# Decode block kernel: first feed-forward and query stage by halves of the heads, a third key tile loaded before it, spare matmuls between output projections, last part of the down weights in two

## The chip, the cores and the metric

One core of one Trainium2 chip runs the whole kernel in one launch. The metric is device time in microseconds (us), less is better. The engines named below: PE (matrix multiply), DVE (vector), ACT (activation), POOL (general), SP (here it only issues loads). PSUM is the memory that PE writes its sums to, in eight banks; SBUF holds everything else.

## The reference, cut to what matters

Four sequences, one new token each, pass twice through an attention block A and a feed-forward block B, with the same weights and the same cache both times.

```python
B, Sq, D = 4, 1, 512;  Hq, Hkv, Sk, Dh = 32, 8, 4096, 128;  F = 1792   # bf16

def A(x):                                  # x is the normalised input
    q = heads(x @ wq)                      # 32 query heads, 4 for each of 8 key heads
    s = q @ k_cache.T * Dh ** -0.5         # 4096 cached keys per key head
    return merge(softmax(s) @ v_cache) @ wo

def Bf(x):
    return (gelu(x @ w_gate) * (x @ w_up)) @ w_down

x = x + A(layernorm(x));  x = x + Bf(layernorm(x))
x = x + A(layernorm(x));  x = x + Bf(layernorm(x))
```

A key head's cache of one sequence is 1 MB, its values another; the kernel reads about 100 MB in all.

## The kernel before, in words

**Tiles.** A key or value tile is half of one head's cache of one sequence, 128 partitions by 16 x 128 numbers, 512 KB. The eight key heads are two groups of four; a group has 8 key tiles (4 heads, t = 0 and 1). SBUF has room for the 16 key tiles of one sequence (`KP`, line 93, in pairs of heads: `kp{g}_{t}_{j}`) and for 8 value tiles (`slots`, line 95). The key tiles of a sequence stay for both of its passes: what was loaded for pass 1 is used again, turned in place, in pass 2 of the same sequence, and only then overwritten with the next sequence's keys.

**Order of the work.** `attend_first` (873) does pass 1 of sequence 0, reads the other weights and does the output projection. Then, for b = 0 to 3, the loop at 1242 does the first feed-forward of sequence b (`dense_first` for b = 0, `dense` after), the queries of its second pass, and `attend(b + 1)` (946), in which pass 2 of sequence b and pass 1 of sequence b + 1 share the engines: scores of the two groups of pass 2 (`sc2`), softmax, values; in between the new keys land, DVE turns them (`Keys.turn`, 483), and the scores of pass 1 (`sc1`) follow, then the remaining values, the output projection (`RowProj`, `OutProj`), and the next feed-forward, in which the remaining values of pass 2 are filled in between (`Streamed`, `prev.fill`).

**Scores** (524). Four heads are computed side by side in four column strips of PE, 32 matmuls of 512 columns for a group: for each t, four parts (`be`) by four heads. They need `qb` (113), a spread-out copy of the queries: `q_sums` (305) makes 16 small matmuls with slices of the identity into PSUM, `q_spread` (314) writes the result times a mask to SBUF on DVE.

**Loads.** All are issued by SP in program order, and a load that overwrites a tile waits for the instructions that still read it. So new keys can be loaded only when the scores of pass 2 have read the old ones, and values only when a slot is free (`VRing.pump`, 628, called around each value step of `Values.step`, 748). An instruction with a wait holds back everything behind it on its engine.

**Around the change.** After the loads of the output, gate, up and down weights (`load_rest`, 139; the down weights in three parts of 6, 5 and 3 of 14 rows, `WD_PARTS`) one pair of new keys (sequence 1, first two heads of the first group, t = 0) is loaded ahead of the feed-forward. To make room, one pair of the second group's t = 1 tiles (`KP[gy2][1][1]`, heads 2 and 3) is copied by DVE into four free PSUM banks (`Parked`, 490; four copies). In `attend`, after the scores of t = 0, ACT copies half of it back to the pair of tiles that these scores have freed, and the other half after the softmax; `KP`'s entries are exchanged. The remaining new keys of the first group are loaded in pairs, one pair after t = 0, two after t = 1; the second group's 8 tiles one by one after its scores (985).

`dense_first` (1109): gate sums (56 matmuls), gelu, up sums (56), product, down sums (56 matmuls in 14 rows). `busy(n)` (439) issues n spare matmuls of 512 columns whose output (`idle`, in the bank of the scores) nobody reads: 6 before the up sums, 4 after, 2 before each later part of the down weights, 1 after the down sums, 1 after the queries and 1 after their sums. The queries of the first group are 64 matmuls (`q_proj`, 249), rounded by DVE (`q_round`, 298); those of the second group are computed after the first softmax (`qy`, 1300).

Of the kernel before, what the change touches and what calls it, by code (L numbers as in the profile page):

```python
# [15 lines left out]
P = 128  # L16
# [13 lines left out]
WD_PARTS = (0, 6, 11, 14)  # L30
# [3 lines left out]
def kernel(  # L34
# [80 lines left out]

    def k_tile(i, t):
        return KP[i // GH][t][i % GH // 2][:, i % 2]

    def acc(shape, name):
        t = ps_ac.tile([P, 512], FP32, name=name, tag="acc")  # L120
        n = 1
        for s in shape:
            n *= s
        if len(shape) == 1:
            return t[:, :n]
        return t[:, :n].rearrange("p (a b) -> p a b", b=shape[1])
# [171 lines left out]
    def q_round(q_bf, q, g, norm):  # L298
        nc.vector.scalar_tensor_tensor(out=q_bf[:], in0=cs_q[:, g], scalar=norm.mean,  # L299
# [4 lines left out]

    def q_sums(q):
        qe = ps_sm.tile([P, GH, BE, rep], FP32, name="qe", tag="sm")
        iv = ident_bf[:].rearrange("p (b w e) -> p b e w", b=NB, e=2)
        for be in range(BE):
            for a in range(QD):
                nc.tensor.matmul(qe[a * QS:(a + 1) * QS, :, be], lhsT=iv[:, be // 2, be % 2],  # L310
                                 rhs=q, start=True, stop=True, skip_group_check=True)
        return qe

    def q_spread(qe):
        dst = qb[:, W:].rearrange("p (n x a h) -> p n x a h", x=2, a=QD, h=rep)[:, :, 0]
        nc.vector.tensor_tensor(  # L316
            out=dst,
            in0=qe.rearrange("p s n h -> p (s n) h").unsqueeze(2).broadcast_to([P, NK, QD, rep]),
            in1=amask.unsqueeze(1).unsqueeze(3).broadcast_to([P, NK, QD, rep]),
# [12 lines left out]
    class OutProj:  # L332


        def __init__(self, o_of, nb):
            self.o, self.nb, self.n = o_of, nb, 0
            self.full = acc([KD, WIDE], "y")
# [49 lines left out]
    def ffn_in(rhs, w_sb, name):  # L387
        g = acc([KF, WIDE], name)
# [48 lines left out]
    idle = []  # L437

    def busy(count):
        if not idle:  # L440
            idle.append(ps_sc.tile([P, 512], FP32, name="idle", tag="sc"))
        for _ in range(count):
            nc.tensor.matmul(idle[0][:], lhsT=ident_bf[:], rhs=wg_sb[:, 0, :512], start=True,
                             stop=True, skip_group_check=True)

    def down(nb, H_bf):
        y = acc([KD, WIDE], "y2")
        for c in range(KF):
            if c in WD_PARTS[1:]:
                busy(2)  # L450
# [6 lines left out]
    class Keys:  # L457
# [16 lines left out]
        def load_pairs(self, count, into=None):  # L474
            for _ in range(count):
                kvh, t = self.tile(self.nl)
                self.nl += 2
# [863 lines left out]
```

## Time and profile before

| | us |
|---|---|
| median of three runs (272.24 to 274.52) | 273.4 |
| the profiled execution, its own time | 271.11 |
| its span, first to last instruction | 269.2 |
| PE busy | 190.0 |
| DVE busy | 174.7 |
| ACT busy | 64.2 |
| POOL busy | 2.7 |
| bytes moved | 103.08 MB, mean 383 GB/s |

How to read it: times in rows are microseconds from the span's start, then the duration, the engine, the line of the kernel (L531 is line 531; a helper's line stands for all its callers), the output and its inputs, the shape, and how often. What stands in brackets is how long the engine was idle before, and what ended that. PEld are weight loads of PE, which overlap its matmuls; SPq is SP's queue of load issues. A row of a stretch of time gives PE, PEld, DVE, ACT and POOL busy time with counts, then the granted clock of PE (1.00 is full), the share of the DMA engines that was busy, and the rate in GB/s. Transfers were above 90% busy in nearly all of the span; PE's clock was granted at full or at half speed, 0.854 on average.

### The profile page before, as it was taken

Reading aid. Unit: us, or ns where it says so; the run is one execution under the profiler, and the core shown is the slowest. Engines: PE = TensorE matmul, PEld = TensorE weight load, DVE = VectorE, ACT = ScalarE, POOL = GpSimd, SP = SyncE. Lnnn points to the kernel's source line nnn. Section 1 sums busy time; section 2 is a strip of 40 time slices with the busy share of each in tenths; the row PEclk is TensorE's granted clock in tenths of the full one; section 3 lists DMA queues with packets and bytes.
Section 4 is the critical chain, followed back from the end, with each engine's and each line's share of the span. In section 5 each row is a group of like instructions: output and inputs, shape, how many; then the busy total and the mean of one; then the engine's idle time right before and its main releaser. Section 6 shows DMA issues by size and latency. Waiting matters only on the chain.

```text
span 269.2 us, 8883 instructions
## 1 busy us (share of the span) xinstructions
PE 190.0 (71%) x3943; PEld 113.8 (42%) x3943; DVE 174.7 (65%) x428; ACT 64.2 (24%) x125; POOL 2.7 (1%) x8
## 2 busy tenths in 40 slices
PE   1395255634597896968869969687788786788893
PEld 1333133633364443544426335454354354453561
DVE  3394952130124799875676999566759995768863
ACT  1001000100404412030422610304137113044640
POOL 2000000000000000000000000000000000000001
PEclk9999559555599798687897997889979979799999
DMA  6999999999993999999999999999999999999940
GB/s 244 421 417 421 418 420 416 413 382 402 411 360 100 419 415 418 420 418 416 402 386 417 417 420 417 416 422 416 412 417 415 417 419 417 416 391 386 417 159 3
DMA packets 32430, 103.08 MB, mean 383 GB/s; under 512 B 2692, under 2 KB 8584, under 8 KB 32392
## 3 DMA queue, kind: packets, MB, share of 16 engines
q1 hardware_dynamic: 32368, 102.51, 95.1%
q8 instruction: 31, 0.51, 0.7%
q14 instruction: 7, 0.06, 0.1%
q10 hardware_dynamic: 24, 0.01, 0.0%
HBM read 102.50 MB, written 0.00 MB: 381 GB/s over the span
## 4 chain that ended last, share of the span: by engine, by line
DMA 51%; DVE 21%; PE 17%; SPq 6%; issue 2%; ACT 1%; DVEq 0%; ACTq 0%
DMA v_t<-in_A_v_cache_dram 29%; DMA kp<-in_A_k_cache_dram 13%; DVE kp L488 10%; PE sc L531 7%; DMA wu_sb<-in_B_w_up_dram 5%; DMA kp<-in_A_v_cache_dram 4%; SPq L142 4%; PE so L712 2%; DVE pe L541 2%; DVE q L280 2%; DVE qb L316 1%; PE ot L779 1%; PE y L246 1%; PE q L274 1%; SPq L143 1%
## 5 line engine op out<-in xcount | busy, mean ns | idle before, releaser
L488 DVE STREAM_TRANSPOSE kp<-kp 128x1024 f32<-128x1024 f32 x64 | 74.0, 1206 | 0.2 <-issue 0.2
L531 PE MATMUL sc<-kp,qb 128*32 128x512 bf16 x512 | 66.6, 449 | 7.5 <-DVE qb L316 2.5
L779 PE MATMUL ot<-pe,v_t 128*128 128x32 bf16 x1120 | 35.3, 181 | 14.4 <-DMA v_t<-in_A_v_cache_dram 12.4
L779 PEld LDWEIGHTS <-v_t 128*128 128x128 bf16 x1120 | 33.1, 99 | 24.2 <-DMA v_t<-in_A_v_cache_dram 15.9
L531 PEld LDWEIGHTS <-qb 128*32 128x32 bf16 x512 | 21.3, 102 | 42.2 <-issue 23.1
L553 ACT ACTIVATE pe<-sc,nl 128x512 bf16<-128x512 f32 x8 | 5.5, 687 | 84.9 <-DVE pe L550 67.2
L583 PE MATMUL x<-pe,ident_bf 128*32 128x128 bf16 x192 | 6.0, 255 | 15.1 <-DVE pe L561 15.0
L583 PEld LDWEIGHTS <-ident_bf 128*32 128x32 bf16 x256 | 5.6, 107 | 18.9 <-issue 17.1
L541 DVE TENSOR_REDUCE pe<-sc 128x1 f32<-128x512 f32 x12 | 8.3, 689 | 7.9 <-PE sc L531 7.9
L720 DVE STREAM_TRANSPOSE so<-so 128x256 f32<-128x256 f32 (+1 forms) x19 | 11.1, 584 | 3.2 <-PE so L712 3.1
L712 PE MATMUL so<-v_t,pe 128*32 128x256 bf16 x192 | 10.2, 341 | 2.8 <-ACT pe L586 1.4
L246 PE MATMUL y<-OT_bf,wo_sb 128*128 128x32 bf16 x192 | 7.3, 190 | 6.8 <-DMA wo_sb<-in_A_wo_dram 6.7
L246 PEld LDWEIGHTS <-wo_sb 128*128 128x128 bf16 x256 | 8.6, 102 | 8.0 <-DMA wo_sb<-in_A_wo_dram 7.1
L586 ACT CAST pe<-x 128x512 bf16<-128x512 f32 x12 | 7.0, 585 | 20.3 <-PE x L583 20.3
L712 PE MATMUL so<-v_t,pl 128*32 128x256 bf16 x192 | 9.7, 283 | 2.9 <-DMA v_t<-in_A_v_cache_dram 2.6
L379 DVE TENSOR_TENSOR xb<-XX,y 128x4 bf16<-128x4 f32 (+1 forms) x9 | 1.6, 173 | 14.2 <-PE y L246 14.1
L246 PE MATMUL q<-xb,wq_sb 128*128 128x5 bf16 (+1 forms) x192 | 5.4, 170 | 7.3 <-DMA wq_sb<-in_A_wq_dram 7.3
L561 DVE STREAM_TRANSPOSE pe<-pe 128x512 bf16<-128x512 bf16 x12 | 8.4, 697 | 3.2 <-ACT pe L553 3.2
L616 DVE TENSOR_TENSOR OT_bf<-ot,rden 128x8 bf16<-128x8 f32 (+1 forms) x20 | 3.0, 156 | 11.1 <-PE ot L779 11.0
L360 PE MATMUL yr<-wo_sb,OT_bf 128*2 128x512 bf16 (+1 forms) x96 | 10.2, 494 | 0.0
L310 PE MATMUL qe<-q_bf,ident_bf 128*32 128x16 bf16 x256 | 4.4, 175 | 8.2 <-DVE q_bf L299 6.3
L712 PEld LDWEIGHTS <-pe 128*32 128x32 bf16 x208 | 6.1, 113 | 8.2 <-issue 3.8
(148 smaller groups left out, 229.6 us busy)
## 6 DMA issues: line engine op xcount, KB each, us to landing
v_t<-in_A_v_cache_dram SPq DMA_DIRECT2D x97, 512.0 KB, 8.9
kp<-in_A_k_cache_dram SPq DMA_DIRECT2D x40, 512.0 KB, 12.4
kp<-in_A_k_cache_dram SPq DMA_DIRECT2D x12, 1024.0 KB, 8.3
wq_sb<-in_A_wq_dram SPq DMA_DIRECT2D x2, 2048.0 KB
wo_sb<-in_A_wo_dram SPq DMA_DIRECT2D x4, 1024.0 KB, 11.4
wq_sb<-in_A_v_cache_dram SPq DMA_DIRECT2D x3, 1024.0 KB, 11.2
wg_sb<-in_B_w_gate_dram SPq DMA_DIRECT2D x1, 1792.0 KB
wu_sb<-in_B_w_up_dram SPq DMA_DIRECT2D x1, 1792.0 KB
```

What stands on the lines that cost most here:

```text
L142: dq.dma_start(out=wo_sb[:, i * n:(i + 1) * n], in_=wo_dram[:, i * n:(i + 1) * n])
L246: nc.tensor.matmul(dst, lhsT=lhsT, rhs=rhs, start=first, stop=last, skip_group_check=True)
L360: nc.tensor.matmul(self.rows[j:j + x.shape[1]], lhsT=x, rhs=wo_sb[:, i], start=self.n < QD, stop=True, skip_group_check=True)
L488: nc.vector.transpose(out=words, in_=words)
L531: nc.tensor.matmul(sc[s * QS:(s + 1) * QS], lhsT=qb[:, w0:w0 + 2 * W], rhs=kt[:, :, be // 2, :, be % 2], start=(t == 0 and be == 0), stop= ...
L541: nc.vector.tensor_reduce(out=m, in_=sc.rearrange("p c j -> p (c j)"), axis=AX.X, op=ALU.min if norm else ALU.max)
L561: nc.vector.transpose(out=flat, in_=flat)
L583: nc.tensor.matmul(x[a * QS:(a + 1) * QS, s], lhsT=ident_bf[:, s * QS:(s + 1) * QS], rhs=pT[:, a], start=True, stop=True, skip_group_check ...
L586: nc.scalar.copy(out=pe, in_=x.rearrange("p s t c h -> p (s t c h)"))
L712: nc.tensor.matmul(ps[d, :NW * QS], lhsT=x[:, w:w + NW].rearrange("p c h -> p (c h)"), rhs=v[:, i:i + NW, d], start=first and i == 0, stop ...
L720: nc.vector.transpose(out=flat, in_=flat)
L779: nc.tensor.matmul(self.ot[:, s % 2], lhsT=v[:, i, :], rhs=wide(pe[:, s, t * CH + i, :]), start=(done == 0 and i == 0), stop=(done == NT - ...
```

## The change

Five edits, of which the first four lie between the end of pass 1 of sequence 0 and the start of the second score group of its pass 2.

1. **Down weights in four parts**: rows 0 to 5, 6 to 10, 11 and 12, 13. Of the spare matmuls in the down sums one is left, before row 6, and it is narrower (384 columns). The one after the down sums and the two around the queries go. Spare matmuls now write into the bank that the next real sums will use, instead of a bank of their own.
2. **Spare matmuls in the first output projection**: `WARM` = 22 of 32 columns, before each of its last three parts, into columns of the same bank that nobody reads.
3. **Three key tiles parked and loaded early** (`Early`): the pair as before (now on the bank pairs h, x and ot, ot), and a third tile in the score bank (a half) and in two SBUF tiles (a quarter each). DVE makes seven copies instead of four. Returning: ACT three half tiles, DVE two, POOL two quarters.
4. **Queries and scores by halves** (`Early.queries`, `Early.scores`): heads 2 and 3 first, then 0 and 1. The queries of the second group (`qy`) are computed between the first run of scores and the second, and four spare matmuls are put ahead of the second group's scores. New keys are loaded one tile at a time: two after the first run, two after the second, one after the third.
5. **Where tiles live** is kept in a dictionary, `place`. After the exchange some pairs of heads are no longer neighbours, and `load_pairs` then issues two single loads, in all later sequences.

The diff, cut to its core:

```diff
-WD_PARTS = (0, 6, 11, 14)
+WD_PARTS = (0, 6, 11, 13, 14)
+WARM = 22
...
-    def busy(count):
...
+    def busy(count, unread, by=None, start=True):
+        rhs = wg_sb[:, 0] if by is None else by
         for _ in range(count):
+            nc.tensor.matmul(unread, lhsT=ident_bf[:], rhs=rhs[:, :unread.shape[1]], start=start,
+                             stop=start, skip_group_check=True)
...
         for c in range(KF):
-            if c in WD_PARTS[1:]:
-                busy(2)
+            if c == WD_PARTS[1]:
+                busy(1, whole[:, KD * WIDE:], start=False)
...
-        def load_pairs(self, count, into=None):
+        def load_pairs(self, count):
             for _ in range(count):
                 kvh, t = self.tile(self.nl)
+                (to, n), (other, m) = place[kvh, t], place[kvh + 1, t]
+                if to is not other or (n, m) != (0, 1):
+                    self.load(2)
+                    continue
...
-        parked = Parked(KP[gy2][NT - 1][1].rearrange("p h c d -> p (h c d)"),
-                        [(ps_h, "h"), (ps_x, "x"), (ps_ot[0], "ot"), (ps_ot[1], "ot")])
-        ahead = Keys(b + 1, (gx2, gy2))
-        ahead.load_pairs(1, into=KP[gy2][NT - 1][1])
+        scr = Scratch()
+        early = Early(b + 1, second_groups[b])
         proj = OutProj(o1(b), 1)
-        for h in pairs(one(b)):
+        for n, h in enumerate(pairs(one(b))):
+            if n:
+                busy(WARM, proj.bank[:, KD * WIDE:KD * WIDE + QS], ident_bf, start=False)
             proj.heads(h, hp)
...
+    class Early:
+        def __init__(self, b, groups):
+            self.gx, self.gy = groups
+            last = NT - 1
+            a, c = self.gx * GH, self.gy * GH
...
+            self.two = [Parked(flat[2], [(ps_h, "h", 2), (ps_x, "x", 2)]),
+                        Parked(flat[3], [(pool, "ot", 2) for pool in ps_ot])]
+            self.one = Parked(flat[1], [(ps_sc, "sc", 2), (pep, "pe", 4), (pep, "pl", 4, 1)])
+            place[a, 0], place[a + 1, 0] = self.own[c + 2, last], self.own[c + 3, last]
+            place[a + 2, 0] = self.own[c + 1, last]
+            self.keys = Keys(b, groups)
+            self.keys.load_pairs(1)
+            self.keys.load(1)
+
+        def queries(self, b, st):
...
+            heads(n, 2 * n)
+            q_round(q_bf, qs[0][:, :, b:b + 1], g, norm, n)
+            qs.append(acc([n, WIDE], "q"))
+            heads(0, n // 2)
+            qe = q_sum_tile()
+            q_sums_of(qe, q_bf[:], half, half)
+            heads(n // 2, n)
+            q_spread(qe, half, half)
+            q_round(q_bf, qs[1][:, :, b:b + 1], g, norm)
+
+            def rest():
+                q_sums_of(qe, q_bf[:], 0, half)
+                q_spread(qe, 0, half)
+                norm.scales()
...
+        def scores(self, sc, qy, norm):
...
+            first([(2, 0), (3, 0)])
+            load(a + 3, 0, (a + 2, 0))
+            load(a, last, (a + 3, 0))
+            self.rest()
+            q = qy()
+            first([(2, last), (3, last), (0, 0), (1, 0)])
+            load(a + 1, last, (a + 2, last))
+            load(a + 2, last, (a + 3, last))
+            to = home(c + 1, last, (a + 1, 0))
+            self.one.back(to, 1, nc.vector)
+            self.one.back(to, 2, nc.gpsimd)
+            self.two[0].back(home(c + 2, last, (a, 0)), 2)
+            first([(0, last), (1, last)])
+            load(a + 3, last, (a, last))
+            to = home(c + 3, last, (a + 1, last))
+            self.two[1].back(to, 1)
+            other = new_scores()
+
+            def build():
+                qe = q_sums(q)
+                busy(4, other.rearrange("p c j -> p (c j)"))
+                q_spread(qe)
+
+            p0 = soft(sc, norm, meanwhile=build)
+            self.two[1].back(to, 1, nc.vector)
+            return p0, other
...
         b0, nb, n = 0, 1, 2 * RUN
...
-        busy(6)
-        u = ffn_in(rhs, wu_sb, "u")
-        busy(4)
+        whole = bank("u")
+        busy(6, whole[:])
+        u = ffn_in(rhs, wu_sb, "u", whole)
+        whole = bank("y2")
+        busy(4, whole[:])
...
-        y = down(nb, H_bf)
-        busy(1)
-        return y
+        return down(nb, H_bf, whole)
...
-            q = queries(gx)
-            busy(1)
-            q_round(q_bf, q, gx, norm)
-            q_build(q_bf[:])
-            busy(1)
+            norm = early.queries(b, st)
```

`home(i, t, freed)` gives tile (i, t) the place of the tile that was just read for the last time, `load` also issues its load there; a and c are the first heads of the first and the second group.

187 lines of the change are left out of this document (110 added, 77 removed).

## The prediction, made before the changed kernel was run

> **What bounds the kernel now.** I read the page's slices first, then sums over stretches of time, then the chain of work that ended last, then the instructions in order of time around the change.
>
> ```profile
> span 269.2 us, 8883 instructions
> GB/s 244 421 417 421 418 420 416 413 382 402 411 360 100 419 415 418 420 418 416 402 386 417 417 420 417 416 422 416 412 417 415 417 419 417 416 391 386 417 159 3
> DMA 51%; DVE 21%; PE 17%; SPq 6%; issue 2%; ACT 1%; DVEq 0%; ACTq 0%
> ```
>
> A slice is 6.73 us. Between the start and the tail transfers run at some 380 to 420 GB/s everywhere but in the twelfth and thirteenth slice; in the latter, 80.8 to 87.5 us, 100 GB/s moved: the hole around which the change is made. The next rows sum stretches of time; their last two numbers are the DMA share and the GB/s.
>
> ```profile
> 79.50:86.75 7.25, 6.05 (x144) 3.66 (x140) 3.17 (x15) 2.43 (x5) 0.00 (x0) 1.00 0.30 85
> 131.00:140.00 9.00, 6.54 (x172) 3.57 (x172) 6.41 (x26) 1.25 (x3) 0.00 (x0) 1.00 1.01 381
> 140.00:190.00 50.00, 39.66 (x780) 22.98 (x781) 38.49 (x86) 14.78 (x27) 0.00 (x0) 0.90 1.03 418
> ```
>
> At 418 GB/s the first stretch would have carried 3.03 MB; it carried 0.62: 5.8 us of transfer time are lost in the hole. From 131 to 140 us the rate is 381, so 0.8 us are lost there: transfers already run as slots come free, not ahead of them. After that they are full again. The chain through the hole, and the instruction that ends it:
>
> ```profile
> 79.34 0.37 PE y L246 x12
> 80.23 1.63 PE q L246 x64
> 81.89 0.24 DVE q_bf L299
> 82.17 0.32 PE qe L310 x16
> 82.51 0.43 DVE qb L316
> 82.99 2.06 PE L531 MATMUL sc<-kp,qb 128*32 128x512 bf16 x32 [0.23 <-DVE qb L316]
> 84.19 0.37 SPq L481 DMA_DIRECT2D kp<-in_A_k_cache_dram  x1
> ```
>
> Down sums, queries, their sums, their spread, scores; with the first key tile's scores done the first load of new keys is issued at 84.19.
>
> **The change, part by part. Down's last part in two.** The last part of the down weights, 384 KB, has these rows (issue, and its time to landing as the last number):
>
> ```profile
> 69.30 3.04 SPq L147 DMA_DIRECT2D wd_sb<-in_B_w_down_dram  x1
> wd_sb<-in_B_w_down_dram SPq DMA_DIRECT2D x1, 384.0 KB, 9.9
> ```
>
> It lands at 69.3 + 9.9 = 79.2. Its 12 matmuls take 0.37 (31 ns each) and start at 79.34, behind two spare ones; they end at 79.71. Now 8 of the 12 belong to a part that lands 0.3 earlier (128 KB at 418 GB/s), no spare ones stand ahead, and 4 x 31 ns follow the last landing: about 79.4. Gain 0.3.
>
> **Queries by halves.** 64 matmuls in 1.63 are 25.5 ns each. Only 32 (0.82) now stand ahead of the first rounding; 16 (0.41) run while DVE rounds (0.24), 16 more while it spreads; the sums still take 0.32, since they are as many. The half spread has 128 elements a partition; between the 0.24 of a rounding (16 elements) and the 0.43 of 256 I take 0.32. Path: 0.82 + 0.41 + 0.32 + 0.41 = 1.96 against 2.76 (80.23 to 82.99). Gain 0.8; with the 0.3, scores start at 81.9.
>
> **Scores in three runs.** What a run costs is seen in the row of 82.99, four heads side by side, and in a later stage with three side by side and the fourth alone.
>
> ```profile
> 112.31 2.06 PE L531 MATMUL sc<-kp,qb 128*32 128x512 bf16 x16
> ```
>
> 32 matmuls by fours are 8 steps; 12 by threes and 4 alone are 8 steps too, and both take 2.06: a step is 0.257 however many heads share it. Two, four and two heads at once need 4 + 4 + 4 steps: 3.09, so 1.03 more in all. The first run ends at 81.9 + 1.03 = 82.9, and the first load goes out at 83.0: 1.2 earlier.
>
> **Third tile early.** 512 KB at 418 GB/s are 1.25 us of transfers moved ahead of the hole. Its issue on SP follows the pair's:
>
> ```profile
> 72.44 1.13 SPq L481 DMA_DIRECT2D kp<-in_A_k_cache_dram  x1
> ```
>
> SP then has nothing to issue until 84.19, so this costs nothing; even some us late it would be ahead of the hole. The hole shrinks from 5.8 to about 5.8 - 1.25 - 1.2 = 3.35: transfers get a lead of 2.45 us.
>
> **What the first stage pays.** Between run one and run two now stand the second half's sums and the query rows of the other group, which came after the stage before. The rows for them and for what follows:
>
> ```profile
> 84.84 1.07 PE L274 MATMUL q<-wq_sb,xb 128*32 128x512 bf16 x16
> 84.14 1.93 ACT L512 COPY kp<-park 128x1024 bf16<-128x1024 bf16 x2 [2.74 <-PE sc L531]
> 85.11 0.70 DVE pe L541
> 86.65 0.78 ACT L553 ACTIVATE pe<-sc,nl,ln 128x512 bf16<-128x512 f32 x1 [0.58 <-DVE pe L550]
> 87.52 0.32 PE qe L310 x16
> 88.21 0.70 DVE L561 STREAM_TRANSPOSE pe<-pe 128x512 bf16<-128x512 bf16 x1
> 88.83 2.33 DVE L488 STREAM_TRANSPOSE kp<-kp 128x1024 f32<-128x1024 f32 x2
> 88.35 3.67 PE sc L531 x27
> 92.04 0.69 DVE pl L541
> L500 DVE TENSOR_SCALAR park<-kp 128x512 int32<-128x512 int32 x4 | 2.5, 682 | 0.0
> ```
>
> The last run ends at 82.95 + 0.32 + 1.07 + 2.06 = 86.4, where the scores ended at 85.05 before. Maximum 0.7 (87.1), the other group's spread 0.43, and the small steps up to the exponential, 0.84 before (85.81 to 86.65): 88.4. ACT has brought back three half tiles by then (85.4 + 3 x 0.97 = 88.3), so the exponential is not held. It ends at 89.2; turning it 0.7 and two key tiles 2.33 ends at 92.2. The second stage's scores are done before that: they begin at 87.6 and take 2.06 at full clock (3.67 before, at half clock: 88.35 to 92.02). So the second maximum starts at about 92.2 instead of 92.04: DVE is 0.2 late, though transfers are 2.45 early. The four spare matmuls into the next score bank (4 x 0.22) run while DVE spreads.
>
> **Off the path.** Parks go from four to seven, at most 0.68 each: 2.0 more, in a stretch in which PE still waits for output weights (next row, the second of four such groups), and DVE is next needed after the fourth. The 66 spare matmuls, 22 in each of three waits for the output weights: the nearest row is
>
> ```profile
> 59.94 1.18 PE L246 MATMUL y<-OT_bf,wo_sb 128*128 128x32 bf16 x32 [1.49 <-DMA wo_sb<-in_A_wo_dram]
> ```
>
> 32 of the same width in 1.18 are 37 ns each, 0.81 a group, inside a wait of 1.49; without those waits they would cost 2.4. Later batches load some pairs as two tiles (rounds of 2 and 4 pairs become 2 pairs with 4 tiles, then 1 pair with 6): five more issues at 0.34 on SP, which waits anyway. POOL's two copies have no row; its rows are these.
>
> ```profile
> 1.01 0.29 POOL masks.py:199 TENSOR_SCALAR_AFFINE_SELECT ident_bf<-ident_bf 128x128 bf16<-128x128 bf16 x1
> 4.42 1.02 POOL L181 TENSOR_TENSOR ln<-ln,masks 128x4 f32<-128x4 f32 x1 [3.12 <-DVE ln L197]
> ```
>
> Low end 0.29 each, high end four times that plus 1.02, 2.2 each; I take 1.2 (four times the 128 elements): from 85.4 to 87.8, and they are needed at 88.6. Even at the high end (89.8) the second scores end at 90.9, ahead of DVE's 92.2.
>
> **Where the lead goes.** From the second maximum to the last stage's scores DVE has no air, and then come the waits that a lead can remove:
>
> ```profile
> 92.00:113.30 21.30, 17.96 (x350) 10.64 (x339) 20.89 (x35) 4.02 (x9) 0.00 (x0) 0.84 1.03 418
> 122.97 0.40 PE L712 MATMUL so<-v_t,pe 128*32 128x256 bf16 x8 [0.24 <-DMA v_t<-in_A_v_cache_dram]
> 124.23 0.57 PE L779 MATMUL ot<-pe,v_t 128*128 128x32 bf16 x16 [0.64 <-DMA v_t<-in_A_v_cache_dram]
> 124.65 0.65 PE L246 MATMUL y<-OT_bf,wo_sb 128*128 128x32 bf16 x16
> 125.46 0.58 PE L779 MATMUL ot<-pe,v_t 128*128 128x32 bf16 x16 [0.16 <-DMA v_t<-in_A_v_cache_dram]
> 126.31 0.59 PE L246 MATMUL y<-OL_bf,wo_sb 128*128 128x32 bf16 x16
> 129.60 0.33 SPq L634 DMA_DIRECT2D v_t<-in_A_v_cache_dram  x1
> ```
>
> DVE is busy 20.89 of 21.30, so its 0.2 carries on. At the end of this batch's attention PE waits 0.24 + 0.64 + 0.16 = 1.04 for values. With values early these waits go, less 0.2 for the lag and 0.3 because the output sums at 124.65 then wait for a turned head: 126.31 becomes about 125.75, a gain of 0.55. Dense work hangs on it, and frees the value slots: the load at 129.60 follows a slot freed there, and here the rate was already below 418. So the lead of 2.45 runs into unfreed slots between 126 and 131, and transfers go on 0.55 early. From 140 on they are full, so 0.55 reaches the end.
>
> **Sum.** 271.11 (this execution: span 269.2 and 1.9 around it) - 0.55 = 270.55. The median shown, 273.4, stands 2.3 above this execution; the same step from it gives 272.8.
>
> **Rivals.** *The whole lead arrives.* If value slots come free earlier than I think, 2.1 to 2.45 survive: about 271.1. For it: transfers are 51% of the chain. Against it: the 381 GB/s, and no more than 1.04 of waits there to remove.
>
> *The clock falls in the first stage* (slower). Spare matmuls that stood between the down parts and around the queries are gone. The granted clock is the last number but two:
>
> ```profile
> 57.00:66.00 9.00, 4.21 (x118) 3.88 (x119) 0.70 (x2) 0.00 (x0) 0.00 (x0) 0.50 1.08 393
> 77.00:79.70 2.70, 2.48 (x61) 1.80 (x61) 0.07 (x1) 0.00 (x0) 0.00 (x0) 1.00 1.04 411
> 85.27:88.68 3.41, 1.25 (x32) 0.45 (x28) 2.87 (x9) 2.79 (x6) 0.00 (x0) 0.95 0.91 317
> ```
>
> PE at 92% busy kept full clock, at 47% it did not win it, and 37% in 85.27 to 88.68 lost it. I count some 73% between 76.9 and 80.3. If the clock is lost there, 12 steps and the query rows cost 3.1 + 1.1 more: lag 4.4, which is 3.9 slower: 277.2. It decides at a lag of 0.75 (no gain) and 3.4 (slower by 1%).
> [...]
>
> *POOL is late* (no gain). Were its copies done only at 92.4, the second scores would end at 93.5, a lag of 1.5: 274.1. POOL's only long calls, 1.02, speak against it.
> [...]
>
> *The third tile isn't early, or doesn't count.* Then the lead is 1.2, still above the 0.55 that can be used: 272.8 too.
>
> **How the numbers follow.** Forecast (with the last rival) 0.45, own range 271.9 to 273.6; whole lead 0.22, around 271.1, half of it past 1%; POOL or another lag of 0.75 to 3 in the first stage 0.18, 273.4 to 275.5, a fifth past 1%; clock 0.15. A measurement of this kernel tells about 1% (2.7 us) from no change. Faster by more: 0.11; slower by more: 0.15 + 0.04 = 0.19; within: 0.70. The range leaves out the clock case and the ends of the others: 270.7 to 275.2.
>
> **What would show it.** First key load after the hole at 83.0, not 84.2; hole 3.35, not 5.8; last run's end at 86.4; second maximum at 92.2; the waits at 123 to 125.5 gone and the last output sums at 125.75; a new dip in the rate between 121 and 131. I am wrong if the second maximum comes before 91.5 (more gain) or after 93 (none), if granted clock in 79 to 89 isn't 1.00, or if the rate stays full up to 131 (whole lead).

## The result, and the profile after

| | this kernel | kernel before |
|---|---|---|
| median of 20 runs each, taken together | 271.38 us (269.26 to 275.42) | 273.62 us (270.73 to 276.46) |
| ratio, 95% interval | 0.9928 [0.9899, 0.9956] | |
| the profiled execution, its own time | 273.38 us | 271.11 us |

The change saves 0.72%, 2.0 us (1.2 to 2.8). The ratio leaves out, of either kernel, the executions more than 1.5% above its fastest, so it is not quite the ratio of the two medians; the profiled execution of this kernel is one of those left out. The forecast was a gain of 0.55, the rival "the whole lead arrives" one of 2.1 to 2.45. The measured gain is the rival's size.

One execution of either kernel lies anywhere between 269 and 276 us. The profiled one of this kernel is 2.0 above its median, that of before 2.5 below its own. So totals are compared by medians, and the two traces only place by place; even there one execution differs from the next. The page of the profile after:

```profile
span 271.6 us, 9070 instructions
PEclk9997559555599777959989989959989899599987
GB/s 256 419 417 421 417 421 417 408 383 406 405 383 276 407 417 419 419 403 358 375 416 419 419 417 417 417 419 372 363 417 417 417 422 415 417 346 392 412 41 1
DMA 44%; DVE 23%; PE 19%; SPq 9%; issue 3%; ACT 2%; DVEq 0%
```

A slice is 6.79 us here. The thirteenth moved 276 GB/s where it moved 100 before. But two dips are deeper: 358 and 375 in the nineteenth and twentieth slice (122 to 136 us; 416 and 402 before), 372 and 363 in the twenty-eighth and twenty-ninth (183 to 197 us; 416 and 412 before), at the dense stages after the first and the second batch. The rates by stretch (last number GB/s), first before, then after:

```profile
76.00:92.00 16.00, 13.19 (x266) 7.11 (x262) 7.94 (x24) 5.32 (x9) 0.00 (x0) 0.89 0.70 264
110.00:145.00 35.00, 27.49 (x580) 15.46 (x575) 22.66 (x66) 7.51 (x16) 0.00 (x0) 0.84 1.02 409
165.00:200.00 35.00, 26.76 (x578) 15.49 (x577) 22.79 (x67) 7.64 (x17) 0.00 (x0) 0.89 1.02 416
```

```profile
76.00:92.00 16.00, 13.77 (x321) 8.94 (x324) 10.21 (x31) 4.91 (x9) 1.17 (x2) 1.00 0.88 342
110.00:145.00 35.00, 27.79 (x586) 16.07 (x583) 22.31 (x71) 8.10 (x18) 0.00 (x0) 0.85 1.01 395
165.00:200.00 35.00, 26.12 (x610) 15.49 (x607) 23.09 (x71) 8.80 (x19) 0.00 (x0) 0.90 1.00 397
```

Against 418 GB/s, the rate from 140 to 190 us before (the stretch times the part of 418 that is missing), the hole costs 16 x 154 / 418 = 5.9 us before and 2.9 after; 35 x 9 / 418 = 0.8 against 1.9 in the second stretch; 0.2 against 1.8 in the third. So about 3.0 us were won in the hole, and in this execution 2.7 of them were given back at the two later boundaries. The same kernel's second profile (the first experiment below) has these rows:

```profile
76.00:92.00 16.00, 14.80 (x340) 9.75 (x337) 9.32 (x28) 4.91 (x9) 1.17 (x2) 0.89 0.76 286
110.00:145.00 35.00, 26.97 (x577) 15.28 (x575) 22.44 (x66) 7.51 (x17) 0.00 (x0) 0.89 1.02 410
165.00:200.00 35.00, 27.96 (x580) 15.91 (x575) 22.23 (x66) 7.51 (x16) 0.00 (x0) 0.85 1.02 405
```

By the same sum that is 5.1, 0.7 and 1.1 us lost: 0.8 won in the hole and about as much given back. So neither the small hole nor the deep dips belong to the kernel as such, and neither trace adds up to the gain of the medians.

The first stage in order of time, kernel after:

```profile
79.10 0.17 DVE L395 TENSOR_TENSOR xb<-XX,y 128x4 bf16<-128x4 f32 x1 [2.40 <-PE y L252]
81.41 0.63 PE L557 MATMUL sc<-kp,qb 128*32 128x512 bf16 x4
82.11 0.40 PE L557 MATMUL sc<-kp,qb 128*32 128x512 bf16 x2
82.12 0.39 PE L324 MATMUL qe<-q_bf,ident_bf 128*32 128x8 bf16 x4
82.45 1.02 PE L280 MATMUL q<-wq_sb,xb 128*32 128x512 bf16 x14
82.54 9.44 SPq L488 DMA_DIRECT2D kp<-in_A_k_cache_dram  x13
83.23 1.57 PE L557 MATMUL sc<-kp,qb 128*32 128x512 bf16 x20
84.57 1.17 POOL L533 COPY kp<-park 128x512 bf16<-128x512 bf16 x2 [79.25 <-DVE q_bf L306]
85.35 0.69 DVE L567 TENSOR_REDUCE pe<-sc 128x1 f32<-128x512 f32 x1
86.42 2.29 PE L557 MATMUL sc<-kp,qb 128*32 128x512 bf16 x32
91.04 0.65 DVE L567 TENSOR_REDUCE pl<-sc 128x1 f32<-128x512 f32 x1
124.84 0.55 PE L252 MATMUL y<-OL_bf,wo_sb 128*128 128x32 bf16 x16
125.43 0.17 DVE L395 TENSOR_TENSOR xb<-XX,y 128x4 bf16<-128x4 f32 x1 [0.64 <-PE y L252]
128.78 0.40 PE L738 MATMUL so<-v_t,pl 128*32 128x256 bf16 x8 [0.81 <-DMA v_t<-in_A_v_cache_dram]
131.15 0.40 PE L738 MATMUL so<-v_t,pl 128*32 128x256 bf16 x8 [0.47 <-DMA v_t<-in_A_v_cache_dram]
```

The row of 79.10 (the sum x + y, the first thing that needs the down sums) is called *the sum*, that of 91.04 *the second maximum*, and that of 125.43 *the next sum*; before they are:

```profile
79.75 0.17 DVE L379 TENSOR_TENSOR xb<-XX,y 128x4 bf16<-128x4 f32 x1 [2.68 <-PE y L246]
92.04 0.69 DVE L541 TENSOR_REDUCE pl<-sc 128x1 f32<-128x512 f32 x1 [0.88 <-PE sc L531]
126.93 0.17 DVE L379 TENSOR_TENSOR xb<-XX,y 128x4 bf16<-128x4 f32 x1 [0.68 <-PE y L246]
```

The scores start at 81.41, the first load goes out at 82.54, the first maximum begins at 85.35, and the second at 91.04, 1.0 earlier than before, where the forecast had it 0.2 later. From the sum to the second maximum, *the first stage*, it took 12.29 before and 11.94 here. The waits for values between 123 and 125.5 are gone in this execution, and ones of 0.81 and 0.47 stand at 128.8 and 131.2.

### The profile page after: what moved, and what is told of

Its sections match the earlier page's. It is cut to its first block, busy times and chain, and to the rows that moved or that the text cites. A ratio compares the mean times of both kernels' runs of the same rounds, so it can differ in the third digit from the quotient of the medians.

```text
span 271.6 us, 9070 instructions
## 1 busy us (share of the span) xinstructions
PE 193.3 (71%) x4020; PEld 117.2 (43%) x4023; DVE 177.2 (65%) x435; ACT 63.4 (23%) x124; POOL 3.9 (1%) x10
## 4 chain that ended last, share of the span: by engine, by line
DMA 44%; DVE 23%; PE 19%; SPq 9%; issue 3%; ACT 2%; DVEq 0%
DMA v_t<-in_A_v_cache_dram 19%; DMA kp<-in_A_k_cache_dram 17%; DVE kp L507 12%; PE sc L557 5%; DMA kp<-in_A_v_cache_dram 5%; SPq L148 4%; DMA wd_sb<-in_B_w_down_dram 4%; SPq L153 3%; PE ot L805 2%; PE so L738 2%; PE q L280 2%; DVE pe L587 1%; PE g L280 1%; PE y L252 1%; DVE q L286 1%
## 5 line engine op out<-in xcount | busy, mean ns | idle before, releaser
L557 PEld LDWEIGHTS <-qb 128*32 128x32 bf16 x512 | 22.3, 103 | 40.4 <-issue 23.0
L738 PE MATMUL so<-v_t,pe 128*32 128x256 bf16 x192 | 9.3, 312 | 4.2 <-DMA v_t<-in_A_v_cache_dram 2.0
L324 PE MATMUL qe<-q_bf,ident_bf 128*32 128x16 bf16 (+1 forms) x272 | 5.5, 175 | 7.6 <-DVE q_bf L306 4.8
L395 DVE TENSOR_TENSOR xb<-XX,y 128x4 bf16<-128x4 f32 (+1 forms) x9 | 1.6, 173 | 12.9 <-PE y L252 12.8
L376 PE MATMUL yr<-wo_sb,OT_bf 128*2 128x512 bf16 (+1 forms) x96 | 9.4, 453 | 0.0
L738 PEld LDWEIGHTS <-pe 128*32 128x32 bf16 x208 | 5.4, 105 | 9.0 <-issue 3.1
```

What stands on the lines that cost most here:

```text
L376: nc.tensor.matmul(self.rows[j:j + x.shape[1]], lhsT=x, rhs=wo_sb[:, i], start=self.n < QD, stop=True, skip_group_check=True)
L557: nc.tensor.matmul(sc[s * QS:(s + 1) * QS], lhsT=qb[:, w0:w0 + 2 * W], rhs=kt[:, :, be // 2, :, be % 2], start=(t == 0 and be == 0), stop= ...
L738: nc.tensor.matmul(ps[d, :NW * QS], lhsT=x[:, w:w + NW].rearrange("p c h -> p (c h)"), rhs=v[:, i:i + NW, d], start=first and i == 0, stop ...
```

## The experiments

Two theories are named in the expectations. These also call some runs by short names: e3 is the kernel without halves, e5 the changed kernel with more vector work, e6 that with the gate weights loaded again, e7 the third tile alone, e10 the spare matmuls put back. By the **compute theory**, on which the forecast rested, the chain of PE and DVE through the first stage reaches the end one for one, and lead of the transfers counts only as far as waits for values go. By the **transfers theory** the kernel before is bound by its transfers, compute has more slack (time by which it can be late without cost) than the forecast saw, and the lead counts nearly whole. Every kernel was run 12 times and compared with 35 runs of the kernel before on the same chip, in three groups on three chips; 0.3 to 0.4% either way is the interval of one ratio. Diffs are against the changed kernel unless said otherwise.

**The changed kernel again** (no edit).

> The changed kernel once more, beside its partial undoings and with a profile of its own. Two theories. Compute: after the hole the time follows the chain on PE and DVE (first stage, second maximum on DVE at 91.0 where it was 92.0, key turns, last stage), and the transfers' lead is lost against value slots that are not yet free, so the gain is the 1.0 of the second maximum plus up to 1.0 of waits for values: 1.0 to 2.0 us. Transfers: the gain is what the hole lost, 5.8 to about 3.4 us: 2.4. Both expect about 2 us faster than before; the profile should show full transfers from 85 to 258 under the transfers theory, and a new dip between 120 and 134 under the compute theory.

0.9945 [0.9912, 0.9977], 272.13 against 273.54. It repeats. Over both samples the changed kernel stands at about 0.9935, 1.8 us faster. Its first stage took 11.94 again, but it began 1.2 later: the granted clock was at half from 76.7 to 80.1, ahead of it.

```profile
80.27 0.17 DVE L395 TENSOR_TENSOR xb<-XX,y 128x4 bf16<-128x4 f32 x1 [2.51 <-PE y L252]
92.21 0.65 DVE L567 TENSOR_REDUCE pl<-sc 128x1 f32<-128x512 f32 x1
126.55 0.17 DVE L395 TENSOR_TENSOR xb<-XX,y 128x4 bf16<-128x4 f32 x1 [0.64 <-PE y L252]
```

So the second maximum is 0.2 later than before here and the next sum 0.4 earlier, and two waits for values, of 0.61 and 0.15, stay ahead of 125.2. Neither sign that was to tell the theories apart came: transfers were not full from 85 to 258 (381 GB/s at 88 to 95, 383 at 183 to 190), and from 110 to 145 they moved 410 GB/s, against 409 before, so there was no new dip.

**Without the third tile**: halves, down in four and the rest stay, only the pair is early.

```diff
-            self.one = Parked(flat[1], [(ps_sc, "sc", 2), (pep, "pe", 4), (pep, "pl", 4, 1)])
-            place[a + 2, 0] = self.own[c + 1, last]
-            self.keys.load(1)
...
-            self.one.back(to, 1, nc.vector)
-            self.one.back(to, 2, nc.gpsimd)
```

> The changed kernel with the third tile neither parked nor loaded early (the pair alone, as before); halves, down in four and spare matmuls stay. 512 KB less are moved ahead of the hole. Compute theory: the second maximum stays at 91 (a DVE copy of 0.7 less ahead of it), so the time stays within 0.3 us of the changed kernel, 2 us faster than before. Transfers theory: 1.25 us slower than the changed kernel, about 0.8 us faster than before.

0.9975 [0.9940, 1.0009]. The third tile is worth about 0.4% of 273.6, 1.1 us, with an error as large. That is near its 1.25 us of transfers (512 KB at 418 GB/s). It speaks against the rival "doesn't count", without excluding it.

**Without halves**: three tiles early, queries and scores in one piece, no spare matmuls put back; the four ahead of the second scores go too, and the second group's queries stand behind the softmax again.

```diff
-            heads(n, 2 * n)
-            q_round(q_bf, qs[0][:, :, b:b + 1], g, norm, n)
...
+            q_round(q_bf, q, g, norm)
+            q_build(q_bf[:])
...
-            first([(2, 0), (3, 0)])
+            first([(s, 0) for s in range(GH)])
```

> The changed kernel with the first group's queries and scores in one piece again (all 64 query matmuls first, scores of t = 0, then of t = 1, the second group's queries after the softmax); the third tile early, down in four and the spare matmuls of the output projection stay. First load after the hole about 1 us later, second maximum at about 92 again. Compute theory: most of the gain goes, 0.3 to 0.9 us faster than before. Transfers theory: the third tile's 1.25 us and the 0.3 of the down sums stay, 1.5 us faster than before.

1.0032 [0.9999, 1.0065]: slower than the changed kernel by 1.0%, 2.6 us, and no faster than before. Its rows are these (sum, second maximum):

```profile
79.52 0.17 DVE L395 TENSOR_TENSOR xb<-XX,y 128x4 bf16<-128x4 f32 x1 [2.36 <-PE y L252]
93.08 0.69 DVE L567 TENSOR_REDUCE pl<-sc 128x1 f32<-128x512 f32 x1 [0.22 <-PE sc L557]
```

13.56 instead of 11.94: the clock fell at 82.3 us here, and DVE waited for the scores (the row's last bracket). Whether the halves were missed, or the clock, the next run but one tells.

**Down in three parts**, two spare matmuls before each later part, as before.

```diff
-WD_PARTS = (0, 6, 11, 13, 14)
+WD_PARTS = (0, 6, 11, 14)
...
-            if c == WD_PARTS[1]:
-                busy(1, whole[:, KD * WIDE:], start=False)
+            if c in WD_PARTS[1:]:
+                busy(2, whole[:, KD * WIDE:], start=False)
```

> The changed kernel with the down weights in three parts and two spare matmuls (384 columns each) ahead of the second and the third part again; all else stays. Down sums end 0.3 to 0.5 us later, and all of the first stage and the first load with them. Both theories: 0.3 to 0.5 us slower than the changed kernel. If it is the same, the split does nothing.

0.9922 [0.9883, 0.9960]: the fourth part and the fewer spare matmuls together bring nothing that can be measured; the edit changes both, so they are not told apart. The sum came at 79.59, in kernels with four parts and one spare matmul mostly at 79.4 to 79.5.

**The third tile alone**: three tiles early, down in three, no halves (as two runs above), and the spare matmuls where they were before.

```diff
+            q = q_proj(lambda k: xb[:, k, :RUN], 1, g)[:, :, b:b + 1]
+            busy(1, spare[0], start=False)
+            q_round(q_bf, q, g, norm)
+            q_build(q_bf[:])
+            busy(1, spare[0], start=False)
```

> The third tile early and parked, with 22 spare matmuls between output projections, but queries and scores in one piece, down in three parts and the spare matmuls of the kernel before (2 and 2 in the down sums, 1 after them, 2 around the queries). It differs from e3 in the spare matmuls and the down parts. In the profile of e3 the granted clock fell at 82.3 us. If the missing spare matmuls did that, this one keeps full clock from 75 to 88 and is about 1.5 us faster than e3: 0.3 to 0.9 us faster than the kernel before by the compute theory, 1.2 by the transfers theory. If e3's loss came from the single tile loads or the later returns, this one is as slow as e3.

0.9943 [0.9905, 0.9981], as good as the changed kernel. Sum and second maximum:

```profile
79.62 0.17 DVE L395 TENSOR_TENSOR xb<-XX,y 128x4 bf16<-128x4 f32 x1 [2.77 <-PE y L459]
91.67 0.69 DVE L567 TENSOR_REDUCE pl<-sc 128x1 f32<-128x512 f32 x1
```

12.05. Beside the kernel without halves (1.0032) this differs only by the spare matmuls (in the down sums, after them and around the queries) and the number of down parts: without halves, these together are worth 0.9% (0.4 to 1.4), 2.4 us. The clock, which fell at 82.3 us there, held to 88.6 here; that it is the reason is likely, not shown. So what slowed the kernel without halves was not the one piece as such. And the run shows that three tiles early are worth something with no halves at all.

**Spare matmuls put back into the changed kernel**: 2, 2 and 1 before the later down parts, 1 after, 1 between queries and scores.

```diff
-            if c == WD_PARTS[1]:
-                busy(1, whole[:, KD * WIDE:], start=False)
+            if c in WD_PARTS[1:]:
+                busy(2 if c < WD_PARTS[3] else 1, whole[:, KD * WIDE:], start=False)
...
+        busy(1, spare[0], start=False)
```

> The changed kernel with spare matmuls back: 2 of 384 columns ahead of rows 6 and 11, one ahead of row 13, one after the down sums, and one between the last query matmuls and the first scores. In four of six profiled executions without those in the down sums the granted clock fell at 80 to 82 us and the second maximum came 13.0 to 13.6 us after the sums' addition; where it did not fall, 11.9. If the lost spare matmuls cost that, this one never loses the clock there and is 0.5 to 1.0 us faster than the changed kernel (ratio about 0.990). If the spare matmuls do not matter, it is the same as the changed kernel or 0.2 us slower.

0.9996 [0.9955, 1.0037]: the gain is lost. The clock stayed full from 73.7 to 94.1 us, but the stage took 12.67 (80.06 to 92.73). Two things lengthen it:

```profile
81.67 0.55 PE L252 MATMUL q<-xb,wq_sb 128*128 128x32 bf16 x16 [0.32 <-DVE q_bf L306]
82.76 0.32 PE L459 MATMUL y<-wg_sb,ident_bf 128*128 128x384 bf16 x1
83.14 0.39 PE L557 MATMUL sc<-kp,qb 128*32 128x512 bf16 x2
```

One is the spare matmul itself, right ahead of the first scores. The other is a wait that the changed kernel doesn't have: 16 query matmuls of the second half wait 0.32 for the rounding of the first half. In the code the spare matmuls keep the bank of the down sums in use beyond the queries, so that the second half has to share a bank with the first; that this is the reason was not tried. From the sum to the query sums it takes 2.09 here (82.15) and 1.62 in the changed kernel (80.72), to the first scores 3.08 and 2.31. So 0.47 of these 0.77 comes from the wait, and this run says little of what spare matmuls placed otherwise would do.

**Halves alone, with those spare matmuls**: the edit of the run above and that of the second run together, only the pair early.

```diff
-            self.keys.load(1)
...
+            busy(1, spare[0], start=False)
```

> Queries and scores by halves and the spare matmuls of e10, but no third tile (the pair alone). With e7 (third tile, no halves, 0.994) and e10 (both) it gives the parts of the gain. Transfers theory: the halves send the first load 1.2 us earlier, 1.2 us faster than before (0.996). Compute theory: the second maximum comes 0.3 us earlier, 0.3 to 0.9 us faster (0.997 to 0.999).

0.9988 [0.9956, 1.0019], stage 12.68 (79.75 to 92.43). With these spare matmuls, and the same wait of 0.32, halves by themselves show no gain. The run above differs from this one by the third tile alone and was timed beside it, 0.9996 against 0.9988: in this pair the third tile shows no worth, with about 0.5% either way.

**No spare matmuls between the output projections.**

```diff
-WARM = 22
+WARM = 0
```

> The changed kernel without the 66 spare matmuls between output projections. In all profiles so far the clock stayed at half speed from 57 to 72 us with them. Expected: the same time as the changed kernel within 0.3 us, and half clock there as well. If they matter, the gate is won later than 75 us without them, and the time is up to 1 us longer.

0.9933 [0.9895, 0.9970], as with them. They do nothing measurable: the clock was at half up to 74.5 us here, and with them up to 75.04. In this execution it fell at 81.3 us. The first two rows are this kernel's, the last two those of the halves with spare matmuls, in the same windows of 3.41 us (last number but two: granted clock):

```profile
77.93:81.34 3.41, 2.86 (x101) 2.56 (x102) 1.09 (x6) 0.41 (x2) 0.00 (x0) 1.00 0.95 385
81.34:84.75 3.41, 3.41 (x60) 1.85 (x56) 0.93 (x5) 0.00 (x0) 0.00 (x0) 0.50 0.09 37
```

```profile
77.93:81.34 3.41, 2.85 (x74) 2.19 (x73) 1.09 (x6) 0.34 (x2) 0.00 (x0) 1.00 0.72 282
81.34:84.75 3.41, 3.33 (x93) 2.54 (x96) 0.93 (x5) 0.07 (x1) 0.00 (x0) 1.00 0.02 5
```

PE was busy equally long in the first window, 2.86 and 2.85 us of 3.41, with 101 and with 74 matmuls, some of the 74 wide spare ones; the first lost the clock, the second kept it.

**More vector work in the changed kernel**: DVE turns the first new key tile twice more, 2 x 1.17 = 2.33 us, ahead of the second maximum.

```diff
+        if early:
+            for _ in range(2):
+                words = k_tile(*keys.tile(0)).rearrange("p c d -> p (c d)").bitcast(FP32)
+                nc.vector.transpose(out=words, in_=words)
```

> The changed kernel with the first new key tile turned three times instead of once, right before DVE turns the new keys after the hole: 2.33 us more on DVE (two turns in 2.33), nothing more on any queue. Compute theory: the last stage of this batch and all behind it come 2.3 us later, so 2.0 to 2.3 us slower than the changed kernel. Transfers theory: transfers are full and ahead, so the delay hides: at most 0.5 us slower.

1.0045 [1.0007, 1.0083]: 1.1% over the changed kernel, 3.0 us (1.8 to 4.2) for 2.33. Second maximum and next sum:

```profile
94.70 0.65 DVE L567 TENSOR_REDUCE pl<-sc 128x1 f32<-128x512 f32 x1
128.15 0.17 DVE L395 TENSOR_TENSOR xb<-XX,y 128x4 bf16<-128x4 f32 x1 [0.64 <-PE y L252]
```

The second maximum is 3.66 later than in the changed kernel's first profile (the clock was at half from 79.96 to 83.38 here, which is a part of it), the next sum 2.7: 0.9 of the lateness had room on the way.

**The same vector work in the kernel before** (its diff is against that).

```diff
+        if parked:
+            for _ in range(2):
+                words = k_tile(*keys.tile(0)).rearrange("p c d -> p (c d)").bitcast(FP32)
+                nc.vector.transpose(out=words, in_=words)
```

> The kernel before with the first new key tile turned three times, 2.33 us more on DVE right before the key turns. Compute theory: the waits for values, 1.04 us at the end of this batch, take up part of it: 1.3 us slower than before (1.005). Transfers theory: hidden, at most 0.3 us slower (1.001). If it costs all 2.3 us (1.0085), DVE and PE were the bound of the kernel before as well.

1.0014 [0.9979, 1.0049]: 0.4 us (-0.6 to 1.3), which reaches from the transfers theory to the 1.3 of the compute theory. The rows say more, second maximum and the next sum:

```profile
93.65 0.65 DVE L541 TENSOR_REDUCE pl<-sc 128x1 f32<-128x512 f32 x1
126.93 0.17 DVE L379 TENSOR_TENSOR xb<-XX,y 128x4 bf16<-128x4 f32 x1 [0.64 <-PE y L246]
```

The second maximum is 1.61 late (0.88 more went into the wait for the scores that stood ahead of it), and the next sum stands where it stood without the extra work, at 126.93. The three waits for values of 0.24, 0.64 and 0.16 ahead of it are gone. So in the kernel before a second maximum 1.6 late had room up to there; in the changed kernel, by the rows of the run above, 0.9. Further on this execution falls back: from 110 to 145 transfers moved 398 GB/s (409 before), and the sum after the next is 1.5 late (183.44 against 181.96). Whether the turns did that is not shown.

**More transfers in the changed kernel**: two quarters of the gate weights are loaded a second time (2 x 448 KB, 2.1 us at 418 GB/s).

```diff
+            dq.dma_start(out=wg_sb[:, 0], in_=B_w_gate.rearrange("(k p) n -> p k n", p=P)[:, 0])
+            dq.dma_start(out=wg_sb[:, 1], in_=B_w_gate.rearrange("(k p) n -> p k n", p=P)[:, 1])
```

> The changed kernel with two quarters of the gate weights (448 KB each) read a second time, right behind the first two key loads after the hole: 2.1 us more of transfers at 418 GB/s, nothing more on the engines. Transfers theory: 2.1 us slower than the changed kernel. Compute theory: the transfers have a lead that is lost anyway, so 0 to 0.6 us slower.

1.0062 [1.0019, 1.0104], but the experiment is flawed: the four spare matmuls ahead of the second scores read one of these quarters, so PE waited for it until 90.8 us; the second scores, which do not read it, stood behind them until 92.62, and the second maximum came at 95.82. It measures that wait, and tells nothing of the theories.

**The same with the up weights**, which no spare matmul reads.

```diff
+            dq.dma_start(out=wu_sb[:, 0], in_=B_w_up.rearrange("(k p) n -> p k n", p=P)[:, 0])
+            dq.dma_start(out=wu_sb[:, 1], in_=B_w_up.rearrange("(k p) n -> p k n", p=P)[:, 1])
```

> e6 with the mistake mended: there the spare matmuls ahead of the second scores read the very quarter of the gate weights that was being loaded again, so PE waited for it. Here two quarters of the up weights (448 KB each) are read a second time at the same place: 2.1 us more of transfers, and no engine reads them before the next feed-forward. Compute alone sets the time: 0 to 0.6 us slower than the changed kernel (ratio 0.993 to 0.996). Transfers alone: 2.1 us slower (1.001). Since two turns more on DVE (e5) already cost about 3 us, a cost of 2 us here would mean that both are tight, and each microsecond on either side counts.

1.0002 [0.9963, 1.0041]: 0.7% over the changed kernel, 1.8 us (0.6 to 3.1) for 2.1. Transfers count in the changed kernel too.

## Why the prediction was right or wrong

The number was in the stated range, but that range was drawn around the rivals as well; the forecast's own, 271.9 to 273.6, does not hold 271.38. In the forecast's sum, 1.04 of waits - 0.2 of lag - 0.3 = 0.55, the term that failed is the lag of **"What the first stage pays"**, and with it the sentence of **"Where the lead goes"** that carries it on one for one. In size the gain is the rival's, "the whole lead arrives"; the rival's own sign, a rate that stays full up to 131, did not come in the profile after. (That half of this rival's case lies past 1%, 2.7 us, didn't follow from its size, 2.45 at most.) By the forecast's own steps:

**Down's last part in two.** 0.3 was counted. Beside 79.75 before, the sum came at 79.1 to 79.7 in the profiles with four parts and one spare matmul, but for the repetition with its half clock: about right for the step as a whole. Three parts with their spare matmuls had 79.59, and the time doesn't change (0.9922).

**Queries by halves.** Right. From the sum to the first score 79.10 to 81.41 is 2.31; before, 79.75 to 82.99 is 3.24: 0.93 less, 0.8 forecast.

**Scores in three runs, and what the first stage pays.** Mis-sized: the second maximum was forecast at 92.2 and came at 91.04. Of these 1.16, 0.5 lie ahead of the first score (81.41, forecast 81.9), which hangs on the early sum. From the first score to the first maximum, 3.94 were measured (81.41 to 85.35) and 4.5 forecast (81.9 to 86.4). The forecast laid first run, sums, query rows and the other runs end to end. In the rows the second half's sums (82.12) run inside the first run, which ends at 82.51, the query rows at 82.45 in its last matmuls, and the next run (83.23) before the rows are over (83.47). So the stage took 11.94 (12.29 before; about 12.8 by the forecast, from a sum at 79.45) in the three executions of the halves where the clock held from the sum on and no spare matmuls stood in the path (this kernel, its repetition, and that with three down parts). Where the forecast has a lag of 0.2, the first of these has a gain of 1.0; the repetition has the 0.2, but only because its stage began late.

**Third tile early.** Right in the profiled execution: the hole went from 5.9 to 2.9 us (3.35 forecast), the first load went out at 82.54 (83.0 forecast). In the repetition the hole was 5.1. POOL's two copies began at 84.57 and took 1.17 together, not 1.2 each, and nobody waited for them: the rival "POOL is late" did not happen. No run shows copies that last until 92.4, the time it takes; here they were done at 85.74.

**Where the lead goes.** DVE's 20.89 of 21.30 us busy between 92 and 113 was read as: a lag there is carried on whole. The extra vector work in the kernel before says otherwise: its second maximum came 1.61 late and the next sum on time. From second maximum to next sum that kernel takes 34.89 (92.04 to 126.93), with the extra work 33.28 (93.65 to 126.93). A DVE that is busy need not be busy with work that is urgent.

The rest of that step held better. From the second maximum to the next sum the changed kernel takes 34.39 in the profile after and 34.34 in the repetition, 0.5 less than before; that is what waits less 0.3 were to bring, 0.74 forecast. Put the measured 1.0 in the place of -0.2 and the forecast's sum gives 1.04 + 1.0 - 0.3 = 1.74; the next sum came 1.5 early (125.43). With the repetition's lag of 0.2 it gives 0.55; there it came 0.4 early (126.55). So up to the next sum the forecast's path holds once its lag is measured. How 0.4 to 1.5 us there become the 1.8 us of the medians at the end stays open: both traces end later than that of before (spans of 271.6 and 271.0 us, 269.2 before).

**What follows it.** The dip in the rate from 121 to 131 came in the profile after as forecast (358 and 375 GB/s up to 136), with a second one at 183 to 197 that did not stand in it. The repetition has next to none of the first (410 GB/s from 110 to 145), so one trace could not have settled it. The rows of the later sums, kernel before and after, in the profiled executions:

```profile
181.96 0.17 DVE L379 TENSOR_TENSOR xb<-XX,y 128x4 bf16<-128x4 f32 x1 [0.64 <-PE y L246]
237.00 0.17 DVE L379 TENSOR_TENSOR xb<-XX,y 128x4 bf16<-128x4 f32 x1 [0.64 <-PE y L246]
260.95 0.18 DVE L379 TENSOR_TENSOR xb<-XX,y 128x16 bf16<-128x16 f32 x1 [0.64 <-PE y L246]
```

```profile
180.05 0.17 DVE L395 TENSOR_TENSOR xb<-XX,y 128x4 bf16<-128x4 f32 x1 [0.68 <-PE y L252]
235.91 0.17 DVE L395 TENSOR_TENSOR xb<-XX,y 128x4 bf16<-128x4 f32 x1 [0.68 <-PE y L252]
262.16 0.18 DVE L395 TENSOR_TENSOR xb<-XX,y 128x16 bf16<-128x16 f32 x1 [0.64 <-PE y L252]
```

The lead is 1.9 at 180 and 1.1 at 236; then this execution takes 26.25 for the last stretch where that of before took 23.95. That isn't the change: the changed kernel with the up weights reloaded took 23.84 there (237.34 to 261.18), and the kernel before with extra turns 25.96. The granted clock goes with it: 1.00 over this stretch in the four executions that took 23.84 to 24.67, 0.87 to 0.96 in all others, which took 24.67 to 26.45. It is the likely reason why this one profile ends later than a kernel that is slower by the medians; it was not tried by itself.

**The clock falls.** Chance 0.15, price 4.4 us of lag. It did fall between 79.9 and 82.4 us in five of the eight profiled executions without spare matmuls in the later down parts, and in none of the others; in the repetition it fell at 76.7, ahead of the stage. The price was mis-sized: the clock came back one window, 3.41 us, later in the four where its return was read, and the second maximum was 1.0 to 1.6 late (stages of 12.96 to 13.56 against 11.94, extra turns taken off). The forecast had charged the whole stage at half rate. In the changed kernel this is part of a spread that the median already holds: with `WARM` the fall came (79.96 us with the extra turns) and stayed out (the profile after), and without it came at 81.3. Its share in the 269 to 276 us between executions was not measured, since no run set where the windows of 3.41 us begin.

**What made the gain, then.** The third tile with the spare matmuls as they were gives 0.9943; the halves with spare matmuls 0.9988; both together without spare matmuls 0.9928 and 0.9945; both with them 0.9996; the halves without the third tile or spare matmuls 0.9975; the third tile with neither 1.0032. The best reading is that the early tile carries the gain as long as the first stage is not lengthened, and that halves do for the first stage what the spare matmuls did, not more. The two ways are not told apart within 0.35%, and the pair with the spare matmuls back (0.9996 and 0.9988) shows no worth of the tile, so this is argued in part. Both theories had a part: extra vector work was nearly free before (0.4 us), and in the changed kernel 2.33 us of it cost about 3.0, and 2.1 us of transfers about 1.8. Not tried by themselves: the single loads that `place` brings in later sequences, and the four spare matmuls ahead of the second scores. No version tried is faster than the changed kernel by more than its interval.

## What to carry to other kernels

An engine that is busy for 98% of a stretch can still have slack, if what it does there waits for transfers further on, as here (DVE 20.89 of 21.30 us in the kernel before, where a second maximum 1.61 late left the next sum at 126.93): before a lag on it is carried one for one, look at the whole distance to the next common point, or put a known piece of extra work on it and see whether that point moves. A lead for transfers and the length of the compute stage that it starts from had to be won together here: the early tile with a stage of 13.56 us gained nothing. Spare matmuls (the six profiled executions with those in the later down parts kept the clock from 79.9 to 82.4 us, five of the eight others lost it) and a shorter path that does without them were rivals for the same gain here, not terms to add. And take a second trace of the same kernel before reading a gain off one: the hole, the dips and the second maximum moved between two executions by 1.2 to 2.2 us, about what the change was worth.

## What the runs showed of the hardware

The clock changes on a grid here: in every execution in which two or more of its changes were read, they lie whole multiples of 3.41 us apart (up at 75.04, down at 92.1, up at 98.94 in the profile after: 5 and 2 windows), and the grid lies elsewhere in the next execution (80.10 in the repetition). What makes the clock fall is not shown. It fell after a window with PE busy 2.86 of 3.41 us (77.93 to 81.34, without the spare matmuls between output projections), and after 3.06 (78.69 to 82.10, without the third tile) and 3.07 (78.07 to 81.48, with the up weights loaded again). The busy time alone does not decide, as the pair of windows above shows (2.86 lost it, 2.85 kept it). The width of the matmuls may (101 narrow ones against 74 with wide ones among them), but that was not tried by itself, and the profile after kept the clock beyond a window with PE busy 3.14 us in 104 matmuls (78.45 to 81.86).

Small matmuls ran beside a score run at next to no cost here: the first run, which uses two of four column strips, took 1.10 us (81.41 to 82.51) with most of the 16 sums of the second half among its matmuls, where four steps of 0.257 are 1.03; such sums took 0.32 by themselves before. Whether the two free strips are what makes room was not tried.
